# Pooled attention and a squared-relu feed-forward in one kernel: the squares of two short chunks move from VectorE to ScalarE, relu comes first in a step, the sums of w_in are spread over eight stages, and the attention of a chunk begins up to four steps sooner

## The chip, the cores and the metric

The kernel runs on one core of a Trainium2 chip. The metric is device time in microseconds (us). A core has five engines that run side by side, each working off its own queue in order: TensorE (PE in the profile, its weight loads PEld), VectorE (DVE), ScalarE (ACT), GpSimd (POOL) and SyncE (SP), which here issues every DMA. They wait for each other through semaphores. An instruction that waits holds up everything behind it in its own queue.

## The reference

```python
k_p = k.reshape(B, H, Sp, 8, D).mean(axis=3)          # B=8 batches, H=8 heads, S=576, D=64, Sp=72
v_p = v.reshape(B, H, Sp, 8, D).mean(axis=3)
scores = np.matmul(q, k_p.transpose(0, 1, 3, 2)) / np.sqrt(D)
attn = np.exp(scores - np.max(scores, axis=-1, keepdims=True))
attn = attn / (np.sum(attn, axis=-1, keepdims=True) + 1e-09)
x = np.matmul(attn, v_p).transpose(0, 2, 1, 3).reshape(B * S, H * D)   # 4608 tokens of 512
h = np.maximum(x @ w_in, 0.0)                                          # w_in 512 x 2048
out = h * h @ w_out                                                    # w_out 2048 x 512
```

## The kernel before

**Chunks and steps.** The 4608 tokens are worked off in ten chunks: 0 to 3 of 384 tokens (the short ones), 4 to 9 of 512. A chunk has 16 steps, one for each 128 columns of `w_in`; step s is step s % 16 of chunk s // 16. Every float32 product is made of three matmuls, with each operand split into a rounded high part and the rest (`gh` and `gl`, the two halves of `x`, `st`, `w_i`).

**A step of a short chunk.** `hidden(c, fc)` puts 12 matmuls into a PSUM bank `h` (two of these banks, shared with `pc` and `pd` below). `activate()` then takes relu and square of the bank into `r`: relu on ScalarE, the square on ScalarE in chunks 0 and 1 and on VectorE in 2 and 3. In the next step `split_hidden` makes `gh` (ScalarE) and `gl` (VectorE) from `r`, and three steps later (two in chunks 0 and 1) `project` multiplies them with `w_out` into the banks `o` (9 matmuls); the weights `ws` come back from DRAM for each step. In the code before, `activate()` is called last in a step, behind all of that step's attention work.

**Long chunks.** From chunk 4 on (`SC = 4`) the hidden layer is computed with a scheme of seven products instead of eight: two steps make one group of columns, with seven products of 6 matmuls (`pc`, `pd`, `pe`), whose operands are blocks of the chunk's `x` (`B11`, `T1` and so on, made by `difference` and `operands`) and sums of blocks of `w_in` (`S1` to `S4`, tile `w_s`). `build(g, stage)` makes these sums for four groups of columns out of `w_i` and scratch tiles `u`: `combine` adds on VectorE, `high` casts on ScalarE, `low` subtracts on VectorE. `first_half` (even steps) and `second_half` (odd steps) write the order of products out by hand. In `first_half` the bank `pc` of the first product is copied to `r1` by ScalarE, and the product with `S2` is then added into the same bank, so TensorE has to wait for that copy.

**Attention ahead of time.** The attention of chunk c runs in the steps of the chunks before it, in four pairs of heads. A pair is a list of stages: `turn_q` (VectorE), `split_q` (ScalarE casts, VectorE subtracts, tile `st`), `scores_0` and `scores_1` (TensorE, bank `sps`, one of two `a` banks; then a copy to `sc` on ScalarE and a maximum `mx` over partitions on GpSimd), `exponents` (VectorE subtracts the maximum, ScalarE takes exp, GpSimd sums: `tot`), `send_sums`, `reciprocals`, `send_reciprocals`, `fetch_reciprocals` (a round trip through DRAM: `rc`, `rr`, `rd`, `rb`), `weigh_values` (TensorE, bank `av`, then a copy to `xf` on ScalarE or to `x`) and `normalise`. Pooled keys make such a trip too (`kp`, `kd`, `kt`), and `turn_k` then turns and splits them (`kf`, `kh`, `kl`).

**What sets the order.** Tables of numbers: `FIRST_OF` and `STEADY` give the step, counted from the start of the chunk, from which each pair runs; `STAGES` and `STEADY_STAGES` give the offset of each stage; `KV_OF` and `KV_STEADY` the steps of keys and values; `BUILD` the first step of each `build`. Within a step the calls come in a fixed order: TensorE's work of the step, then the streams of `ws`, the evictions of the scores and values (`later`), the operands, the end of a pair of steps (`finish`), and all other stages in `others()`:

```python
        for f in later:
            f()
        if c < SC:
            urgent()
        if finish:
            finish()
        if c < SC or "t" not in (ORDER_A, ORDER_B)[fc % 2]:
            others()
```

Each engine's queue is then exactly this program order; only the buffers behind the names are given out by the framework.

Of the kernel before, what the change touches and what calls it, by code (L numbers as in the profile page):

```python
# [37 lines left out]
def pooled_attn_relu2_ffn(  # L38
# [24 lines left out]
    NPAIR = H // 2  # L63
# [13 lines left out]
    SC, MC = 4, 2  # L77
    LAG, FLAG, QL = 2, 3, 4
# [1 line left out]
    IDLE = (10, 3)  # L80
    STB, SCB, LD, XB, RB = 1, 3, 2, 7, 3
    ORDER_A, ORDER_B = "1ooo265uao", "7oo3uooa4"
    BUILD, RING = (36, 45, 64, 69), 2


    FIRST, EAGER, AHEAD = 4, 10, 4
    PRO, RATE, MARGIN = 5, 2, 1
# [2 lines left out]


    EARLY = (-16, -13, -10, -6)
    FIRST_OF = {2: (-18, -15, -11, -8), 3: (-20, -17, -13, -10)}
    STEADY = (-24, -20, -16, -12)
    STAGES = {c: (-1, 0, 1, 1, 3, 4, 5, 5, 5, 7) for c in (2, 3)}
    STEADY_STAGES = [(-2, -1, 1, 2, 3, 5, 6, 7, 8, *x) for x in ((11, 12), (8, 9), (7, 9), (7, 9))]
    NKT = H * SP_ // QT
    KV_OF = {3: ((-34, -33, -32, -31, -30, -29), -28, -27, -26, (-26, -25, -24, -23, -22, -21), -20, -19),
             4: ((-32, -31, -30, -29, -28, -27), -26, -26, -24, (-24, -23, -22, -21, -20, -19), -18, -17)}
    KV_STEADY = ((-31, -30, -30, -29, -29, -28), -28, -26, -24, (-24, -23, -22, -21, -20, -19), -18, -17)  # L100
    WC = 256

    const = ctx.enter_context(tc.tile_pool(name="const", bufs=1))
# [482 lines left out]
    def hidden(c, fc):  # L586
        hp = ps_h.tile([P, 512], F32, name=f"h_{c}_{fc}", tag="h")
        cb, o = fc * P // WC, fc * P % WC
        prods = []
        for cc in range(NCC):  # L590
            key, cols = ("i", cb, cc // 2 * 2), slice(cc % 2 * WC + o, cc % 2 * WC + o + P)
            if c == 0 and fc < SPLIT:
                prods += [(wf[key][:, cols], x0[cc // 2][:, cc % 2, :])]
            else:
                prods += [(wt[key][:, w, cols], xts[c][cc][:, x, :]) for w, x in ((0, 0), (0, 1), (1, 0))]
        for i, (w, x) in enumerate(prods):
            PE.matmul(hp[:, :SIZES[c]], lhsT=w, rhs=x, start=i == 0, stop=i == len(prods) - 1)

        def activate():
            if c == 0:  # L600
                r = sb.tile([P, SIZES[c]], F32, name=f"r_{c}_{fc}", tag="gh", bufs=LAG + 1)
            else:
                r = sb.tile([P, SIZES[c]], F32, name=f"r_{c}_{fc}", tag="r", bufs=RB)
            ACT.activation(r, hp[:, :SIZES[c]], AF.Relu)
            if c < 2:
                ACT.activation(r, r, AF.Square)
            else:
                DVE.tensor_tensor(r, r, r, op=ALU.mult)
            gts[c, fc] = r

        return activate
# [22 lines left out]
    def build(g, stage):  # L634
        a11, a12, a21, a22 = (wt["i", g + 4 * r, 2 * k] for r in range(2) for k in range(2))
        hi, lo = (lambda t: t[:, 0, :].bitcast(F32)), (lambda t: t[:, 1, :].bitcast(F32))

        def high(n, src):
            t = wt["s", n, g] = w_tile(F32R, f"w_s{n}_{g}")
            ACT.copy(t[:, 0, :], src)  # L640

        def low(n, src):
            t = wt["s", n, g]
            DVE.tensor_tensor(t[:, 1, :], src, hi(t), op=ALU.subtract)

        def combine(dst, first, second, add):
            DVE.tensor_tensor(dst, first, second, op=ALU.add if add else ALU.subtract)

        if stage == 0:
            us[g] = [half_tile("u", f"u{i}_{g}") for i in range(2)]  # L650
        u1, u2 = us[g]
        if stage == 0:
            combine(u1, hi(a21), lo(a21), True)
            combine(u2, hi(a22), lo(a22), True)
        elif stage == 1:
            combine(u2, u1, u2, True)
            high(1, u2)
        elif stage == 2:
            combine(u1, hi(a11), u1, False)
            combine(u1, u1, lo(a11), True)  # L660
            low(1, u2)
            high(3, u1)
        elif stage == 3:
            combine(u2, u2, hi(a11), False)
            combine(u2, u2, lo(a11), False)
            high(2, u2)
        elif stage == 4:
            low(3, u1)
            low(2, u2)
        elif stage == 5:  # L670
            combine(u2, hi(a12), u2, False)
            combine(u2, u2, lo(a12), True)
            high(4, u2)
        else:
            low(4, u2)
# [142 lines left out]
    def at(step, f, *a):  # L818
        work.setdefault(max(step, -PRO), []).append((f, a))
# [115 lines left out]
                at(k_turn, turn_k, b)  # L935
        at(v_fetch, fetch_rows, "v", b)

    ready = {0, 1}
    stages = (turn_q, split_q, scores_0, scores_1, exponents, send_sums, reciprocals, send_reciprocals, fetch_reciprocals, weigh_values, normalise)
    for c in range(1, NCH):  # L940
        first = EARLY if c == 1 else FIRST_OF.get(c, STEADY)
        offsets = [(0, 1, 2, 3, 5)] * NPAIR if c == 1 else [STAGES[c]] * NPAIR if c in STAGES else STEADY_STAGES
        names = (transpose_q, token_scores, token_normalise, token_turn, weigh_values) if c == 1 else stages
        for b, _, _ in segments(c):
            if b not in ready:
                ready.add(b)
                kv_steps(b, c)
        for p in range(NPAIR):
            s = c * NFC + first[p]
            if c > 1 or p:  # L950
                at(s - QL, load_q, c, p)
            for d, f in zip(offsets[p], names):
                at(s + d, f, c, p)

# [4 lines left out]
        if c >= MC:  # L959
            at(s - (4 if s < SC * NFC - 4 else RING), stream, c, f)  # L960
    for g, s in enumerate(BUILD):
        for stage in range(7):
            at(s + stage, build, g, stage)
    for c in range(SC, NCH):
        s = c * NFC
        for d, f, *names in ((-10, difference, "T1"), (-2, operands, "B11", "B21", "T1"), (-2, difference, "T2"),
                             (-2, operands, "T2"), (-1, difference, "T3"), (-1, operands, "T3"),
                             (-1, difference, "T4"), (-1, operands, "B22"), (0, operands, "T4")):
            at(s + d, f, c, *names)
# [3 lines left out]
    for s in range(-PRO, max(projects) + 1):  # L973
        todo = work.get(s, [])

        def on_array():
            return [f(*a) for f, a in sorted(((f, a) for f, a in todo if f in on_pe), key=lambda x: x[0] is weigh_values)]

        def urgent():
            for f, a in todo:  # L980
                if f in (operands, difference):
                    f(*a)

        def others():
            for f, a in todo:
                if f not in on_pe + last + (stream, operands, difference):
                    f(*a)

        groups = project(*projects[s]) if s in projects else iter(())
        activate = finish = None  # L990
        c, fc = steps[s] if 0 <= s < len(steps) else (0, 0)
        if c < SC:
            activate = hidden(c, fc) if 0 <= s < len(steps) else None
            later = on_array()
            for _ in groups:
                pass
            if 0 <= s - 1 < len(steps) and steps[s - 1][0] < SC:
                split_hidden(*steps[s - 1])
            if s == len(steps):
                high(NCH - 1, NQD - 1)  # L1000
                low(NCH - 1, NQD - 1)
                rest(NCH - 1, NQD - 1)
                low(NCH - 1, NFC - 1)
        else:
            qd = fc // 2
            pc, pq = (c, qd - 1) if qd else (c - 1, NQD - 1)
            before = (pc, pq) if pc >= SC else None
            if fc % 2:
                later, finish = second_half(c, qd, before, groups, on_array, urgent, others)
            else:  # L1010
                if pc < SC:
                    split_hidden(pc, NFC - 1)
                later = first_half(c, qd, before, groups, on_array, urgent, others)
        for f, a in todo:
            if f is stream:
                f(*a)
        for f in later:
            f()
        if c < SC:
# [5 lines that stand above are left out]
        keys = [a[0] for f, a in todo if f is to_float32]  # L1025
        if keys:
            to_float32(*keys)
        for f, a in todo:
            if f is split_weights:
                f(*a)  # L1030
        issue_loads()
        if activate:
            activate()
# [30 lines left out]
```

## Time and profile before

| | |
|---|---|
| median of three runs | 1056.6 us (1050.52 to 1059.32) |
| profiled execution: time, span | 1054.14 us, 1052.4 us |
| mean granted TensorE clock | 0.951 |
| TensorE busy | 942.4 us (90%) |
| VectorE busy | 689.2 us (65%) |
| ScalarE busy | 500.3 us (48%) |
| GpSimd busy | 345.0 us (33%) |

In the lines of the profile below, a group of instructions reads: engine, operation, tiles written <- tiles read, shapes, count, busy time and mean duration, then the idle time of the engine in front of them and what ended it ("<-ACT r" is an instruction of ScalarE on tile `r`). All lines of this kernel carry the number L34, that of a recording helper, so instructions are told apart by their tiles. Tile names lose their buffer numbers: `h`, `pc`, `pe`, `r`. PEclk is the share of its full clock that TensorE was granted. A busy TensorE also runs slower where that share is below 1.

### The profile page before, as it was taken

To read this page: it belongs to the slowest core of one execution; us is meant where nothing else is said; L and a number is where in the kernel's file an instruction comes from. 1 tells how busy PE (TensorE), PEld (TensorE's weight loads), DVE (VectorE), ACT (ScalarE), POOL (GpSimd) and SP (SyncE) were. 2 spreads that over 40 slices of the span, in tenths; PEclk is the share of its full clock that TensorE was granted. 3 is DMA by queue.
4 is the path that set the end of the run, shared out by engine and by line. 5 is a ranking of instruction groups with operands and counts; after the bars stand their busy time and mean duration, and the time that the engine had idled before them with its cause. 6 is when DMAs were issued, how large, how long until landed. Compare 5 with 4: busy or idle time off the path is not lost.

```text
span 1052.4 us, 14702 instructions
## 1 busy us (share of the span) xinstructions
PE 942.4 (90%) x5256; PEld 784.2 (75%) x5256; DVE 689.2 (65%) x1076; ACT 500.3 (48%) x1035; POOL 345.0 (33%) x183
## 2 busy tenths in 40 slices
PE   7899989988887887877779987999799979999998
PEld 6557667876766776766668876887688868888997
DVE  6989776666776577777767667777756565435332
ACT  2897755543343333434345445544554445435333
POOL 4800143443443444223334432443234434300000
PEclk9999999998988988888889999999999999999999
DMA  9953244576364545242435554555443434434701
GB/s 261 340 179 90 66 141 140 189 196 157 104 173 124 133 127 157 94 112 74 117 87 171 146 129 116 171 136 141 106 141 101 123 79 141 120 111 135 286 1 41
DMA packets 144753, 143.54 MB, mean 136 GB/s; under 512 B 98536, under 2 KB 103784, under 8 KB 144680
## 3 DMA queue, kind: packets, MB, share of 16 engines
q1 hardware_dynamic: 144680, 142.60, 46.8%
q8 instruction: 41, 0.67, 0.3%
q14 instruction: 32, 0.26, 0.1%
HBM read 122.72 MB, written 19.72 MB: 135 GB/s over the span
## 4 chain that ended last, share of the span: by engine, by line
PE 36%; DVE 8%; ACT 4%; DMA 3%; issue 1%; SPq 1%; DVEq 0%; ACTq 0%
PE o L34 17%; PE pc L34 9%; PE pe L34 5%; PE pd L34 2%; DVE gl L34 2%; DVE st L34 1%; DVE r L34 1%; PE av L34 1%; DMA vd<-vp 1%; PE sps L34 1%; ACT st L34 1%; DVE xf L34 1%; ACT sc L34 1%; ACT r L34 1%; DMA ws<-wd 1%
## 5 line engine op out<-in xcount | busy, mean ns | idle before, releaser
L34 PE MATMUL o<-ws,gh 128*128 128x512 f32 x960 | 310.4, 405 | 5.6 <-DMA ws<-wd 5.6
L34 POOL PARTITION_ALL_REDUCE tot<-sc x64 | 199.0, 3155 | 150.9 <-ACT sc L34 148.0
L34 POOL PARTITION_ALL_REDUCE mx<-sc x64 | 113.3, 1790 | 406.0 <-DMA rc<-tot 194.9
L34 PEld LDWEIGHTS o<-ws,gh 128*128 128x128 f32 x960 | 171.7, 195 | 36.4 <-issue 6.4
L34 PE MATMUL o<-ws,gl 128*128 128x512 f32 x480 | 191.6, 399 | 2.8 <-DVE gl L34 2.8
L34 PE MATMUL h<-x,w_i 128*128 128x384 f32 x696 | 143.9, 357 | 21.7 <-ACT r L34 21.7
L34 DVE TENSOR_TENSOR gl<-r,gh 128x512 fp32r<-128x512 f32 (+1 forms) x144 | 121.7, 845 | 56.6 <-ACT gh L34 55.0
L34 PEld LDWEIGHTS h<-x,w_i 128*128 128x128 f32 x696 | 129.1, 197 | 34.6 <-ACT r L34 25.4
L34 PE MATMUL pc<-T,w_s 128*128 128x256 f32 x576 | 92.5, 300 | 35.3 <-ACT r L34 35.1
L34 ACT CAST gh<-r 128x512 fp32r<-128x512 f32 (+1 forms) x144 | 84.2, 585 | 77.1 <-DVE r L34 67.5
L34 PEld LDWEIGHTS pc<-T,w_s 128*128 128x128 f32 x576 | 85.4, 206 | 42.4 <-ACT r L34 37.9
L34 PEld LDWEIGHTS o<-ws,gl 128*128 128x128 f32 x480 | 92.8, 193 | 26.6 <-DVE gl L34 5.5
L34 DVE TENSOR_TENSOR st<-qt,st 64x512 fp32r<-64x512 f32 (+1 forms) x64 | 70.0, 1094 | 47.7 <-ACT st L34 46.6
L34 DVE TENSOR_TENSOR r<-pd,r 128x256 f32<-128x256 f32 x48 | 20.3, 423 | 97.8 <-PE pd L34 96.1
L34 ACT COPY r<-pc 128x256 f32<-128x256 f32 x96 | 35.7, 372 | 86.6 <-PE pc L34 86.2
L34 ACT ACTIVATE r<-r 128x512 f32<-128x512 f32 (+2 forms) x128 | 67.3, 526 | 2.5
L34 ACT COPY sc<-sps 72x512 f32<-72x512 f32 (+1 forms) x64 | 34.6, 552 | 48.6 <-PE sps L34 48.5
L34 ACT ACTIVATE sc<-sc 72x512 f32<-72x512 f32 (+1 forms) x64 | 36.6, 601 | 33.1 <-DVE sc L34 33.1
L34 PE MATMUL pc<-T,w_i 128*128 128x256 f32 x288 | 44.8, 291 | 6.7 <-DVE r L34 6.6
L34 PEld LDWEIGHTS pc<-T,w_i 128*128 128x128 f32 x288 | 38.2, 189 | 15.6 <-DVE r L34 10.1
L34 PEld LDWEIGHTS pd<-B,w_i 128*128 128x128 f32 x288 | 41.0, 192 | 11.4 <-ACT r L34 8.1
L34 PE MATMUL pd<-B,w_i 128*128 128x256 f32 x288 | 43.0, 286 | 6.8 <-ACT r L34 6.8
(117 smaller groups left out, 1473.3 us busy)
## 6 DMA issues: line engine op xcount, KB each, us to landing
ws<-wd SPq DMA_DIRECT2D x128, 512.0 KB
k<-in_k_dram SPq DMA_DIRECT2D x48, 192.0 KB
out_dram<-ob SPq DMA_DIRECT2D x36, 256.0 KB
raw_i<-in_moe_w_in_dram SPq DMA_DIRECT2D x16, 512.0 KB
raw_o<-in_moe_w_out_dram SPq DMA_DIRECT2D x16, 512.0 KB
wd<-w_o SPq DMA_DIRECT2D x16, 512.0 KB
v<-in_v_dram SPq DMA_DIRECT2D x36, 192.0 KB
rb<-rd SPq DMA_DIRECT2D x48, 128.0 KB
```

What stands on the lines that cost most here:

```text
L34: return lambda *a, **k: self.tc.keep_in_program_order(f(*a, **k))
```

## The change

The squares of chunks 2 and 3 are taken by ScalarE's Square. In the short chunks except the first, `activate()` is called right behind the streams, ahead of `later` and `others()`. `build` has eight stages instead of seven: a cast of ScalarE now stands a stage, and so a step, behind the sum that it reads. `BUILD` starts two of the four builds one or two steps sooner. The tables of the attention start pairs up to four steps sooner (`FIRST_OF` gets an entry for chunk 4), turn and split the queries of chunks 2 and 3 one step sooner relative to the scores, and fetch and turn pooled keys up to two steps sooner. A load of queries is not put ahead of the step in which the tile before it is turned.

```diff
-    BUILD, RING = (36, 45, 64, 69), 2
+    BUILD, RING = (36, 45, 62, 68), 2
-    STEADY = (-24, -20, -16, -12)
+    STEADY = (-26, -22, -18, -14)
...
             ACT.activation(r, hp[:, :SIZES[c]], AF.Relu)
-            if c < 2:
+            if c < SC:
                 ACT.activation(r, r, AF.Square)
             else:
                 DVE.tensor_tensor(r, r, r, op=ALU.mult)
...
         elif stage == 1:
             combine(u2, u1, u2, True)
+            combine(u1, hi(a11), u1, False)
+        elif stage == 2:
             high(1, u2)
-        elif stage == 2:
-            combine(u1, hi(a11), u1, False)
             combine(u1, u1, lo(a11), True)
+        elif stage == 3:
+            high(3, u1)
             low(1, u2)
-            high(3, u1)
-        elif stage == 3:
             combine(u2, u2, hi(a11), False)
             combine(u2, u2, lo(a11), False)
+        elif stage == 4:
             high(2, u2)
-        elif stage == 4:
             low(3, u1)
+        elif stage == 5:
             low(2, u2)
-        elif stage == 5:
             combine(u2, hi(a12), u2, False)
             combine(u2, u2, lo(a12), True)
+        elif stage == 6:
             high(4, u2)
         else:
             low(4, u2)
...
-                at(s - QL, load_q, c, p)
+                at(max(s - QL, turned), load_q, c, p)
+                turned = s + offsets[p][0]
...
         for f, a in todo:
             if f is stream:
                 f(*a)
+        if activate and c:
+            activate()
+            activate = None
         for f in later:
             f()
```

The first place is ScalarE's queue in chunk 3, around the exponents of the last pair of chunk 4 (`sc_3`): steps 53 to 55. Before, with the relu of a step behind that step's exponents and query casts:

```order
L34 CAST gh_5_3335<-r_5_3305 128x384
L34 COPY sc_3_3297<-sps_3_1_3321 72x512
L34 ACTIVATE r_6_3360<-h_6_3308 128x384
L34 CAST gh_6_3391<-r_6_3360 128x384
L34 COPY xf_2_3376<-av_2_3377 128x512
L34 ACTIVATE sc_3_3297<-sc_3_3297 72x512 x2
L34 CAST st_0_3408<-qt_0_3357 64x512 x2
L34 ACTIVATE r_7_3413<-h_7_3363 128x384
```

The same exponents in ScalarE's queue after the change:

```order
L34 CAST gh_4_3310<-r_4_3268 128x384
L34 ACTIVATE r_5_3316<-h_5_3283 128x384
L34 ACTIVATE r_5_3316<-r_5_3316 128x384
L34 COPY xf_0_3126<-av_1_3296 128x512
L34 ACTIVATE sc_3_3218<-sc_3_3218 72x512 x2
L34 CAST st_0_3338<-qt_0_3280 64x512 x2
L34 CAST gh_5_3371<-r_5_3316 128x384
L34 ACTIVATE r_6_3377<-h_6_3343 128x384
L34 ACTIVATE r_6_3377<-r_6_3377 128x384
```

The relu of a step now stands ahead of the exponents and casts of that step, the square (`r<-r`) stands behind it on ScalarE, and the exponents of this pair come two steps sooner.

The second place is ScalarE's queue where chunk 5 begins (step 79 into step 80). Before, with the exponents of a pair of chunk 6 (`sc_1`) and the casts of the next pair (`st_2`) in the last step of chunk 4:

```order
L34 CAST T_5_4880<-xf_0_4054 128x512
L34 CAST B_5_4884<-xf_2_4342 128x512
L34 ACTIVATE r_15_4819<-pc_7_4775 128x256
L34 ACTIVATE sc_1_4763<-sc_1_4763 72x512 x2
L34 CAST st_2_4915<-qt_2_4857 64x512 x2
L34 COPY r_0_4929<-pc_0_4922 128x256
```

The same place after the change:

```order
L34 CAST T_5_4907<-xf_0_4025 128x512
L34 CAST B_5_4911<-xf_2_4316 128x512
L34 COPY sc_2_4933<-sps_2_0_4920 72x512
L34 ACTIVATE r_15_4847<-pc_7_4803 128x256
L34 COPY r_0_4953<-pc_0_4946 128x256
```

Between the relu of the old chunk's last group and the copy `r<-pc` of the new chunk's first, the exponents and the casts are gone (they now stand in steps 77 and 81); a copy of scores has come ahead of the relu.

The third place is ScalarE's queue in chunk 4, around the sums for the third group of columns (`w_s_2` is the cast `high`). Before, steps 67 into 68:

```order
L34 ACTIVATE r_9_3988<-pc_1_3939 128x256
L34 ACTIVATE sc_2_3922<-sc_2_3922 72x512 x2
L34 CAST st_3_4082<-qt_3_4008 64x512 x2
L34 CAST w_s_2_4092<-u_2_3875 128x512
L34 COPY r_2_4102<-pc_2_4095 128x256
```

After the change, the same exponents, steps 65 into 66:

```order
L34 ACTIVATE r_8_3892<-pc_0_3852 128x256
L34 ACTIVATE sc_2_3828<-sc_2_3828 72x512 x2
L34 CAST st_3_3960<-qt_3_3910 64x512 x2
L34 CAST w_s_2_3968<-u_2_3781 128x512
L34 COPY r_1_3981<-pc_1_3974 128x256
```

The queue reads alike, but the sum `u` that the cast reads was made in the same step before and is made in the step ahead of it now.

More of the change, by code (lines that the diff above doesn't have):

```diff
@@ L92, in pooled_attn_relu2_ffn @@
     EARLY = (-16, -13, -10, -6)
-    FIRST_OF = {2: (-18, -15, -11, -8), 3: (-20, -17, -13, -10)}
-    STEADY = (-24, -20, -16, -12)
-    STAGES = {c: (-1, 0, 1, 1, 3, 4, 5, 5, 5, 7) for c in (2, 3)}
-    STEADY_STAGES = [(-2, -1, 1, 2, 3, 5, 6, 7, 8, *x) for x in ((11, 12), (8, 9), (7, 9), (7, 9))]
+    FIRST_OF = {2: (-18, -15, -11, -8), 3: (-21, -17, -14, -11), 4: (-24, -21, -18, -14)}
+    STEADY = (-26, -22, -18, -14)
+    STAGES = {2: [(-2, -1, 1, 1, 3, 4, 5, 5, *x) for x in ((6, 7), (6, 7), (6, 8), (6, 7))],
+              3: [(-2, -1, 1, 1, 3, 4, *x) for x in ((5, 6, 6, 9), (5, 6, 6, 8), (6, 6, 7, 9), (6, 6, 7, 9))]}
+    STAGES[4] = [(-2, -1, 1, 2, 3, 5, 6, 7, *x) for x in ((8, 10, 11), (8, 10, 11), (8, 8, 9), (8, 9, 10))]
+    STEADY_STAGES = [(-2, -1, 1, 2, 3, 5, 6, 7, *x) for x in ((8, 12, 13), (9, 11, 12), (8, 8, 9), (8, 9, 10))]
     NKT = H * SP_ // QT
-    KV_OF = {3: ((-34, -33, -32, -31, -30, -29), -28, -27, -26, (-26, -25, -24, -23, -22, -21), -20, -19),
-             4: ((-32, -31, -30, -29, -28, -27), -26, -26, -24, (-24, -23, -22, -21, -20, -19), -18, -17)}
-    KV_STEADY = ((-31, -30, -30, -29, -29, -28), -28, -26, -24, (-24, -23, -22, -21, -20, -19), -18, -17)
+    KV_OF = {3: ((-34, -33, -32, -31, -30, -29), -28, -27, -25, (-26, -25, -24, -23, -22, -21), -20, -19),
+             4: ((-32, -31, -31, -30, -30, -29), -29, -28, -26, (-24, -23, -22, -21, -20, -19), -18, -17)}
+    KV_STEADY = ((-31, -30, -30, -29, -29, -28), -28, -27, -26, (-24, -23, -22, -21, -20, -19), -18, -17)
     WC = 256
@@ L936, in kv_steps @@
         at(v_fetch, fetch_rows, "v", b)
-    ready = {0, 1}
+    ready, turned = {0, 1}, -PRO
     stages = (turn_q, split_q, scores_0, scores_1, exponents, send_sums, reciprocals, send_reciprocals, fetch_reciprocals, weigh_values, normalise)
@@ L941, in pooled_attn_relu2_ffn @@
         first = EARLY if c == 1 else FIRST_OF.get(c, STEADY)
-        offsets = [(0, 1, 2, 3, 5)] * NPAIR if c == 1 else [STAGES[c]] * NPAIR if c in STAGES else STEADY_STAGES
+        offsets = [(0, 1, 2, 3, 5)] * NPAIR if c == 1 else STAGES.get(c, STEADY_STAGES)
         names = (transpose_q, token_scores, token_normalise, token_turn, weigh_values) if c == 1 else stages
@@ L961, in pooled_attn_relu2_ffn @@
     for g, s in enumerate(BUILD):
-        for stage in range(7):
+        for stage in range(8):
             at(s + stage, build, g, stage)
@@ L965, in pooled_attn_relu2_ffn @@
         s = c * NFC
-        for d, f, *names in ((-10, difference, "T1"), (-2, operands, "B11", "B21", "T1"), (-2, difference, "T2"),
+        for d, f, *names in ((-9, difference, "T1"), (-2, operands, "B11", "B21", "T1"), (-2, difference, "T2"),
                              (-2, operands, "T2"), (-1, difference, "T3"), (-1, operands, "T3"),
```

## The prediction

> **What bounds the kernel now.** I read the stretches first, one for each chunk that the change touches, and beside them stretches of the same chunks in which TensorE never stops.
>
> ```profile
> span 1052.4 us, 14702 instructions
> core 0: us, PE busy (x) PEld busy (x) DVE busy (x) ACT busy (x) POOL busy (x), PEclk, DMA share, GB/s
> 129.17:211.51 82.34, 77.41 (x365) 63.47 (x364) 56.97 (x87) 46.62 (x95) 32.58 (x17) 0.98 0.50 160
> 148.60:176.41 27.81, 27.81 (x139) 23.68 (x138) 19.84 (x30) 14.11 (x29) 11.23 (x6) 1.00 0.58 178
> 211.51:311.09 99.58, 82.33 (x373) 68.46 (x372) 71.05 (x103) 36.70 (x75) 42.88 (x20) 0.90 0.58 154
> 311.09:409.30 98.21, 82.01 (x401) 69.92 (x399) 67.16 (x91) 36.54 (x71) 41.43 (x16) 0.93 0.48 134
> 381.15:409.30 28.15, 27.86 (x147) 24.32 (x145) 20.71 (x28) 11.29 (x22) 14.07 (x6) 1.00 0.60 169
> 409.30:542.06 132.76, 104.34 (x583) 89.71 (x584) 93.65 (x136) 53.82 (x109) 40.61 (x16) 0.86 0.38 105
> 498.06:510.29 12.23, 12.23 (x80) 10.41 (x79) 10.81 (x17) 5.38 (x12) 3.88 (x2) 1.00 0.49 131
> 542.06:560.02 17.96, 13.35 (x73) 11.78 (x72) 14.07 (x18) 8.10 (x16) 7.98 (x3) 0.81 0.36 99
> 665.99:678.32 12.33, 12.33 (x80) 10.41 (x79) 8.05 (x12) 6.50 (x15) 3.56 (x2) 1.00 0.66 201
> 856.98:874.47 17.49, 12.87 (x71) 11.23 (x70) 13.08 (x17) 8.09 (x16) 7.97 (x3) 0.90 0.33 82
> ```
>
> The rows at 129.17, 211.51, 311.09 and 409.30 are chunks 1, 2, 3 and 4 whole. The row at 148.60 is six consecutive steps of chunk 1 and that at 381.15 the last six of chunk 3 (six times 21 matmuls of the hidden layer are 126; the rest of the 139 and 147 is attention): 27.81 / 6 = 4.64 us and 28.15 / 6 = 4.69 us a step with TensorE full at full clock, attention included. The row at 498.06 is such a pair of steps of chunk 4, that at 665.99 one of chunk 6. The rows at 542.06 and 856.98 are the first pair of chunks 5 and 8, the first and the last of four alike (chunks 5 to 8).
>
> So where TensorE isn't stopped it is the bound, and the cost of a chunk is its clean steps plus stops. At clean steps chunk 1 would be 16 x 4.64 = 74.2 us, chunks 2 and 3 16 x 4.69 = 75.1 each, chunk 4 8 x 12.23 = 97.8, a first pair 12.3. Each loss has two parts. Chunk 2 is 24.5 us over: TensorE stands idle for 99.58 - 82.33 = 17.3, and its busy time is 82.33 instead of 75.1, which goes with the granted clock of 0.90 there. Chunk 3 is 23.1 over (16.2 idle, 6.9 slower busy time), chunk 4 34.9 (28.4 and 6.5), chunk 1 8.2 (4.9 and 3.2). So a stop costs about 1.4 times its length.
>
> Second, the waits, with sum, count and longest, to see what the stops are.
>
> ```profile
> PE pc L34 <- ACT r L34: 35.4, 11, 6.3
> PE h L34 <- ACT r L34: 21.7, 8, 6.2
> PE sps L34 <- DVE st L34: 12.6, 5, 4.2
> PE o L34 <- DMA ws<-wd: 5.6, 2, 4.7
> ACT gh L34 <- DVE r L34: 67.5, 26, 7.4
> DVE gl L34 <- ACT gh L34: 55.0, 60, 5.3
> ACT w_s L34 <- DVE u L34: 41.4, 12, 5.3
> POOL mx L34 <- DMA rc<-tot: 194.9, 25, 14.4
> ```
>
> TensorE waits mostly for ScalarE's `r`, though ScalarE is busy only 48%: `r` is not slow, it stands behind instructions that themselves wait for VectorE.
>
> **The change part by part.** *Relu first.* The window at the start of chunk 4 shows the stop at its longest; the last two rows, some steps earlier, are a sum of GpSimd with a square inside it:
>
> ```profile
> 418.59 0.49 ACT L34 ACTIVATE r<-h 128x384 f32<-128x384 f32 x1
> 419.14 1.65 PE L34 MATMUL pd<-B,w_i 128*128 128x256 f32 x6 [6.81 <-ACT r L34]
> 367.76 6.60 POOL L34 PARTITION_ALL_REDUCE tot<-sc  x2 [2.31 <-ACT sc L34]
> 371.30 2.48 DVE L34 TENSOR_TENSOR r<-r 128x384 f32<-128x384 f32 x1
> ```
>
> The relu at 418.59 empties the bank of chunk 3's last step and is 0.49 us long; `pd` takes that bank and has stood for 6.81 us. Once the relu leads its step, the bank is free about 0.5 us behind its last matmul, and the exponents behind it delay no bank. This answers the 21.7 us of `h` and the 6.81.
>
> *Squares.* What goes from VectorE and comes to ScalarE:
>
> ```profile
> L34 DVE TENSOR_TENSOR r<-r 128x384 f32<-128x384 f32 x32 | 25.6, 799 | 7.6 <-ACT r L34 7.4
> L34 ACT ACTIVATE r<-r 128x384 f32<-128x384 f32 x32 | 16.8, 525 | 1.0
> ```
>
> Sixteen squares a chunk leave VectorE: 16 x 0.80 = 12.8 us, so chunk 2 has 58.3 us of it left in 75.1 and chunk 3 54.4. ScalarE takes 16 x 0.525 = 8.4 more: 45.1 in chunk 2, 60% of 75.1. Chunk 1 already runs so, with ScalarE 14.11 busy in its clean 27.81. I cost the squares at nothing: `gh` is needed two to three steps after the bank is read, so the 0.525 lies beside TensorE; without that cover it would be 32 x 0.525 = 16.8. What it saves is the round trip ScalarE, VectorE, ScalarE, the 67.5 us that `gh` waits for `r`, part of which becomes the stops on `h`.
>
> The square at 371.30 took 2.48 us, inside the GpSimd sum from 367.76 to 374.36, against a mean of 0.80. The Trainium skill, "SBUF — State Buffer", section "Who interferes with whom", says that a VectorE instruction with two SBUF inputs contends with a GpSimd instruction that reads SBUF, and that the other one blocks. The overlap here agrees. By this rule the blocking isn't removed with the square but falls on the next two-input instruction (`gl`, `st`, `kl`); the ScalarE time of 0.525 as the unblocked size leaves 32 x (0.80 - 0.525) = 8.8 us, and the forecast would be that much higher if all of it stood in front of TensorE.
>
> *Sums of `w_in` in eight stages.*
>
> ```profile
> 452.98 0.62 ACT L34 CAST w_s<-u 128x512 fp32r<-128x512 f32 x1 [5.26 <-DVE u L34]
> 453.51 0.36 ACT L34 COPY r<-pc 128x256 f32<-128x256 f32 x1
> 453.93 1.65 PE L34 MATMUL pc<-T,w_s 128*128 128x256 f32 x6 [6.34 <-ACT r L34]
> 516.32 2.62 DVE L34 TENSOR_TENSOR w_s<-u,w_s 128x512 fp32r<-128x512 f32 x1
> 519.00 0.34 SPq L34 DMA_DIRECT2D ws<-wd  x1
> 522.73 1.22 PE L34 MATMUL o<-ws,gh 128*128 128x512 f32 x2 [4.75 <-DMA ws<-wd]
> 524.03 4.04 SPq L34 DMA_DIRECT2D q<-in_q_dram  x8
> ```
>
> ScalarE reached the cast and stood 5.26 us for a sum of the same step; the 0.36 us copy of `pc` behind it kept TensorE 6.34 us. A like stop falls at 482. With the sum a step ahead, the cast finds it done. What could be late next is the sum's own start: two builds start one or two steps sooner and one stage longer, on a VectorE that works 10.81 of 12.23 us in the clean pair. Of a stage, as many sums, casts and differences are issued as before. The stop at 518 is a stream of `ws` issued at 519.00, behind the difference that ended at 518.94: that difference stood behind exponents and queries in step 75, which now stand in 73 and 77. All three stops go in my sum.
>
> *Attention sooner.* Pairs shift so that exponents and query splits fall on steps 1, 5, 9, 13 of a chunk instead of 3, 7, 11, 15.
>
> ```profile
> 547.56 1.23 ACT L34 ACTIVATE sc<-sc 72x512 f32<-72x512 f32 x2 [2.82 <-DVE sc L34]
> 548.70 1.24 ACT L34 CAST st<-qt 64x512 fp32r<-64x512 f32 x2
> 549.97 0.37 ACT L34 COPY r<-pc 128x256 f32<-128x256 f32 x1
> 550.39 1.65 PE L34 MATMUL pc<-T,w_s 128*128 128x256 f32 x6 [4.62 <-ACT r L34]
> ```
>
> Here a chunk's first copy of `pc` stands behind exponents, which wait for VectorE, and casts of the step before it; four chunks pay for it with about 17.7 - 12.3 = 5.4 us each, 21.6 in all. Exponents of step 77 are done a pair before that copy. Of a later pair the same work then stands in step 1 (odd), where no copy of `pc` is waited for by the first product; I cost it at nothing, as in the middle of the chunk, where the clean pair at 665.99 runs.
>
> Moved along are the DMAs. SP issues a load of queries in 4.04 us (eight DMAs), and streams of `ws` queue behind it. Streams come first in a step, and the load stays two steps ahead of its use. Between nothing and the 4.75 us of the row at 522.73 for each load, I take nothing, since a single such stop exists now. GpSimd's maxima and sums come with the pairs; their number stays. The copy of `av` into `xf` falls into the step of the output stores:
>
> ```profile
> 678.23 0.59 ACT L34 COPY xf<-av 128x512 f32<-128x512 f32 x1 [3.17 <-DMA out_dram<-ob]
> 377.21 0.36 PE L34 MATMUL sps<-st,kl 128*72 128x256 f32 x1 [3.06 <-DVE kl L34]
> ```
>
> It already waits 3.17 us for a store, on a ScalarE with idle time; one step earlier it waits longer, and may then hold the relu or copy of the next step. Between nothing and the 3.17 us again in front of TensorE, once a chunk, I take nothing, as the row at 678.23 lies in a stretch that TensorE runs through. Pooled keys are turned two steps sooner and their scores too, so the trip through DRAM gets no longer lead: the 3.06 us of `kl` stays or doubles.
>
> *Sum.* Chunk 1 -8.2, chunk 2 -24.5, chunk 3 -23.1, chunk 4 -34.9, four first pairs -21.6: together -112.3. The profiled execution took 1054.1 us (1.7 over its span), so 941.8 if no stop were left in these places. The four rows of TensorE's waits hold 26 waits; 112.3 / 26 = 4.3 us for each, clock included. I leave six: the pooled keys of chunk 4, the head of chunk 4 (two schemes meet there), and four, one in each of chunks 1 to 4, where VectorE's blocked instruction meets a new neighbour. 941.8 + 6 x 4.3 = **968 us**. The six are a choice, between none (942) and half of the 26 (998). The profiled execution lies 0.2% under the median of 1056.6 and within the runs, so I don't shift the sum.
>
> **The rivals.** *VectorE becomes the bound.* For it: chunk 4 has 93.65 us of VectorE's time and a clean length of 97.8, 96%, and instructions that GpSimd blocks. Against it: the clean pairs ran with 10.81 of 12.23 beside full TensorE, and chunk 2 would be at 78%. If half of the loss in chunks 2 to 4 stays: 41.3 back on 941.8, 983; with two of the six other waits 992.
>
> *ScalarE's longer queue is what TensorE waits for.* The square now stands ahead of score copies and `gh`; if that costs chunks 2 and 3 what they gain, 941.8 + 47.6 = 989. Against it stands chunk 1, clean with the square on ScalarE. The Trainium skill, "ScalarE: Activation LUTs", section "Rules for kernel authors", tells one to take relu and multiplications on VectorE rather than ScalarE. The rows here have 525 ns on ScalarE and 799 on VectorE in this form, so the trace doesn't bear it out.
>
> *Attention does not start sooner.* GpSimd's maxima wait 194.9 us in 25 waits for an earlier pair's sums on their way through DRAM. If that trip, not the tables, sets the pace, exponents stay where they are beside the first pairs, and half of chunk 4's loss with them: 941.8 + 21.6 + 17.5 = 981.
>
> *Slower.* The loads of queries come, in chunks 0 to 4, to stand in front of the stream that TensorE needs next. From the point where a stream's lead falls under the load's 4.04 us, each of 20 loads costs the 4.75 us of the row at 522.73 times 1.4, 6.6: 968 + 132 = 1100. Against it: one such stop now among 40 loads.
>
> **How the numbers follow.** The forecast 0.62, VectorE 0.18, ScalarE 0.10, attention 0.06, slower 0.04. The range from 940 (no stop left) to 1005 (half of the stops left, 998, and a late store or two) holds the first four but for tails. A measurement of this kernel cannot tell less than about 1% from no change; within it I put 0.02, slower 0.04, faster 0.94.
>
> **What would show it.** Chunks 2 and 3 within 76 to 84 us each, at a clock above 0.95; chunk 4 at 98 to 107; first pairs of chunks 5 to 8 at 12.3. In the waits, `h` for `r`, `gh` for VectorE's `r` and `w_s` for `u` should be nearly gone; VectorE about 25 us less busy, ScalarE 17 more. Wrong if TensorE's waits for `st`, `kl` or `gl` grow to tens of us (VectorE), if `h` or `sps` waits for ScalarE's `r` or `sc` (its queue), if first pairs keep 17.7 (attention), or if `o` waits for `ws` in many steps (loads).

## The result and the profile after

The changed kernel takes **982.6 us** (median of three, 979.77 to 984.56) against 1056.6 before: ratio 0.9307, 95% interval 0.9233 to 0.938. The forecast was 968, the range 940 to 1005. In the profiled executions TensorE stands idle for 978.1 - 920.7 = 57.4 us instead of 110.0, and its 5256 matmuls take 920.7 us instead of 942.4, at a mean granted clock of 0.984 instead of 0.951. So 52.6 us less of stops came with a span shorter by 74.3, 1.4 times as much, the factor that the prediction had taken.

The same views of the changed kernel: first the page's head, then the stretches of chunks 1, 2, 3, 4 and 5 (the columns are those of the table in the prediction), the first pairs of steps of chunks 5 and 8, and TensorE's waits with VectorE's and ScalarE's beside them.

```profile
span 978.1 us, 14676 instructions
PE 920.7 (94%) x5256; PEld 766.4 (78%) x5256; DVE 674.8 (69%) x1044; ACT 510.5 (52%) x1067; POOL 345.2 (35%) x183
129.90:205.31 75.41, 75.25 (x365) 62.53 (x363) 60.34 (x89) 47.85 (x101) 37.67 (x18) 1.00 0.57 177
205.31:282.91 77.60, 75.19 (x376) 64.53 (x375) 58.09 (x87) 40.84 (x86) 38.12 (x18) 0.98 0.70 185
282.91:371.46 88.55, 79.18 (x402) 67.59 (x400) 65.73 (x76) 45.48 (x89) 47.76 (x19) 0.96 0.54 155
371.46:486.73 115.27, 99.67 (x585) 84.84 (x584) 93.87 (x135) 54.48 (x111) 42.97 (x17) 0.94 0.46 127
486.73:589.14 102.41, 96.02 (x595) 81.77 (x594) 75.86 (x106) 50.78 (x104) 40.99 (x16) 1.00 0.51 144
486.73:498.16 11.43, 11.31 (x73) 9.87 (x72) 8.81 (x15) 6.00 (x13) 3.17 (x2) 1.00 0.42 138
788.50:799.98 11.48, 11.35 (x70) 9.62 (x69) 9.28 (x17) 6.00 (x13) 3.10 (x2) 1.00 0.14 51
...
ACT gh L34 <- DVE r L34: 10.7, 5, 2.4
PE o L34 <- DVE gl L34: 9.9, 11, 2.9
PE pc L34 <- ACT r L34: 9.1, 12, 3.9
PE pc L34 <- DVE r L34: 7.3, 6, 1.6
PE o L34 <- DMA ws<-wd: 4.4, 3, 1.9
PE sps L34 <- ACT xf L34: 4.1, 1, 4.1
PE sps L34 <- DVE st L34: 2.9, 2, 2.0
PE sps L34 <- DVE kl L34: 2.9, 2, 2.5
ACT w_s L34 <- DVE u L34: 2.3, 2, 1.7
```

Chunks 1 and 2 are now at the pace of their clean steps: TensorE is idle for 0.2 and 2.4 us. The waits of `pc` for ScalarE's `r` fell from 35.4 to 9.1 us, that of `h` for `r` (21.7) is gone from the list, that of ScalarE's cast `w_s` for `u` fell from 41.4 to 2.3 and that of `gh` for VectorE's `r` from 67.5 to 10.7. But chunk 3 still has 88.55 - 79.18 = 9.4 us of idle TensorE and chunk 4 15.6, and two waits of TensorE are new or larger: `o` for `gl` (2.8 us before) and `sps` for the copy into `xf` (none before). These are the places, from the timeline (start, duration, engine, instruction, idle time before it):

```profile
303.60 1.38 SPq L34 DMA_DIRECT2D out_dram<-ob  x3
308.58 0.58 ACT L34 COPY xf<-av 128x512 f32<-128x512 f32 x1 [6.03 <-DMA out_dram<-ob]
309.22 0.44 PE L34 MATMUL sps<-st,kl 128*72 128x192 f32 x1 [4.05 <-ACT xf L34]
...
380.47 0.36 ACT L34 COPY r<-pc 128x256 f32<-128x256 f32 x1
380.88 1.65 PE L34 MATMUL pc<-T,w_s 128*128 128x256 f32 x6 [3.93 <-ACT r L34]
...
447.09 2.43 DVE L34 TENSOR_TENSOR st<-qt,st 64x512 fp32r<-64x512 f32 x2 [1.21 <-ACT st L34]
449.54 2.64 DVE L34 TENSOR_TENSOR w_s<-u,w_s 128x512 fp32r<-128x512 f32 x1
452.21 0.69 DVE L34 TENSOR_TENSOR u<-w_i,u 128x512 f32<-128x512 f32 x1
452.94 0.69 DVE L34 TENSOR_TENSOR u<-u,w_i 128x512 f32<-128x512 f32 x1
453.55 0.41 DVE L34 TENSOR_TENSOR r<-pd,r 128x256 f32<-128x256 f32 x1
453.88 0.68 DVE L34 TENSOR_TENSOR gl<-r,gh 128x512 fp32r<-128x512 f32 x1
454.62 0.80 PE L34 MATMUL o<-ws,gl 128*128 128x512 f32 x1 [2.90 <-DVE gl L34]
...
485.91 0.98 PE L34 MATMUL pc<-T,w_i 128*128 128x256 f32 x6 [1.58 <-DVE r L34]
```

At 308.58 ScalarE's copy into `xf` stood 6.03 us for the output stores: in the kernel `ob`, which they read, and `xf` take turns in the same two buffers. The scores, which need the bank that this copy empties, stood 4.05. At 453.88 `gl` stands in VectorE's queue behind the query split and three operations of a stage of the `w_in` sums. The last row is a short stop in the last step of chunk 4, which comes back at the end of chunks 5 to 7; before, the same stops were 0.93 to 1.31 us long. The row at 380.88 is the head of chunk 4, one of the six stops that the forecast left.

### The profile page after: what moved, and what is told of

Its sections match the earlier page's. It is cut to its first block, busy times and chain, and to the rows that moved or that the text cites. A ratio compares the mean times of both kernels' runs of the same rounds, so it can differ in the third digit from the quotient of the medians.

```text
span 978.1 us, 14676 instructions
## 1 busy us (share of the span) xinstructions
PE 920.7 (94%) x5256; PEld 766.4 (78%) x5256; DVE 674.8 (69%) x1044; ACT 510.5 (52%) x1067; POOL 345.2 (35%) x183
## 4 chain that ended last, share of the span: by engine, by line
PE 55%; DVE 20%; ACT 8%; DMA 7%; issue 5%; SPq 3%; POOL 1%; DVEq 0%; ACTq 0%
PE o L34 26%; PE pc L34 9%; PE h L34 8%; DVE gl L34 5%; PE pe L34 4%; SPq L34 3%; DVE st L34 3%; PE av L34 3%; DVE r L34 2%; PE sps L34 2%; DMA k<-in_k_dram 2%; PE pd L34 2%; ACT r L34 2%; ACT sc L34 2%; ACT st L34 2%
## 5 line engine op out<-in xcount | busy, mean ns | idle before, releaser
L34 POOL PARTITION_ALL_REDUCE mx<-sc x64 | 113.8, 1799 | 366.7 <-DMA rc<-tot 193.3
L34 DVE TENSOR_TENSOR gl<-r,gh 128x512 fp32r<-128x512 f32 (+1 forms) x144 | 130.5, 906 | 28.3 <-ACT gh L34 26.9
L34 PE MATMUL h<-x,w_i 128*128 128x384 f32 x696 | 136.6, 345 | 0.0
L34 PEld LDWEIGHTS h<-x,w_i 128*128 128x128 f32 x696 | 123.9, 188 | 9.9 <-issue 4.8
L34 PE MATMUL pc<-T,w_s 128*128 128x256 f32 x576 | 87.4, 288 | 9.2 <-ACT r L34 9.1
L34 ACT CAST gh<-r 128x512 fp32r<-128x512 f32 (+1 forms) x144 | 84.2, 585 | 18.1 <-DVE r L34 10.7
L34 PEld LDWEIGHTS pc<-T,w_s 128*128 128x128 f32 x576 | 79.3, 193 | 17.2 <-ACT r L34 13.4
L34 DVE TENSOR_TENSOR st<-qt,st 64x512 fp32r<-64x512 f32 (+1 forms) x64 | 66.0, 1031 | 38.7 <-ACT st L34 37.5
L34 ACT ACTIVATE r<-r 128x384 f32<-128x384 f32 (+2 forms) x160 | 84.1, 526 | 3.5
L34 DVE TENSOR_TENSOR r<-pd,r 128x256 f32<-128x256 f32 x48 | 20.2, 421 | 83.8 <-PE pd L34 83.4
L34 ACT ACTIVATE r<-pc 128x256 f32<-128x256 f32 x48 | 18.4, 383 | 81.9 <-PE pc L34 81.7
L34 PE MATMUL pc<-T,w_i 128*128 128x256 f32 x288 | 44.1, 289 | 7.3 <-DVE r L34 7.3
L34 ACT COPY r<-pe 128x256 f32<-128x256 f32 x48 | 17.9, 373 | 62.5 <-DVE gl L34 53.5
L34 DVE TENSOR_REDUCE kp<-k 96x64 f32<-96x512 f32 x42 | 43.5, 1054 | 7.6 <-DMA k<-in_k_dram 7.4
```

What stands on the lines that cost most here:

```text
L34: return lambda *a, **k: self.tc.keep_in_program_order(f(*a, **k))
```

## The experiments

Twelve kernels, each timed in four runs, with its own runs of the kernel before on the same chip. Totals are compared through those. Lengths of chunks come from one profiled execution each, from the first product of a chunk to the first of the next; they leave out the time ahead of chunk 0's first product, which wandered between 41.1 and 44.1 us (50.9 in the last kernel) whatever was changed. The length of a chunk wanders too: chunk 2 has the same instructions in the same order in the changed kernel and in the three kernels "sums a step later", "values a step later" and "both later", and took 77.6, 80.1, 79.2 and 78.2 us. So a difference of 2 to 3 us in one chunk means nothing, and one of about 4 is weak evidence.

| kernel | ratio to before (95%) | chunk 1 | 2 | 3 | 4 | 5 to 8 |
|---|---|---|---|---|---|---|
| before | | 82.3 | 99.6 | 98.2 | 132.8 | 413.1 |
| the change | 0.931 (0.923 to 0.938) | 75.4 | 77.6 | 88.5 | 115.3 | 394.3 |
| relu first alone | 0.983 (0.977 to 0.988) | 85.8 | 92.5 | 90.5 | 126.8 | 412.7 |
| squares alone | 0.985 (0.981 to 0.990) | 81.9 | 95.3 | 91.7 | 126.3 | 412.9 |
| eight stages alone | 0.980 (0.975 to 0.984) | 83.5 | 93.6 | 93.0 | 121.3 | 415.1 |
| attention tables alone | 0.964 (0.960 to 0.968) | 75.4 | 98.1 | 103.0 | 119.4 | 393.5 |
| all but relu first | 0.932 (0.929 to 0.936) | 75.4 | 82.6 | 91.1 | 110.8 | 396.2 |
| all but the squares | 0.943 (0.940 to 0.947) | 75.4 | 83.6 | 95.6 | 116.2 | 395.6 |
| all but eight stages | 0.942 (0.937 to 0.946) | 75.4 | 82.0 | 92.0 | 122.9 | 396.2 |
| all but the tables | 0.964 (0.961 to 0.967) | 86.6 | 87.4 | 83.7 | 116.2 | 415.7 |
| sums a step later | 0.931 (0.928 to 0.934) | 75.4 | 80.1 | 90.1 | 115.0 | 394.1 |
| values a step later | 0.931 (0.929 to 0.934) | 75.4 | 79.2 | 92.5 | 114.4 | 393.8 |
| both later | 0.928 (0.925 to 0.932) | 75.4 | 78.2 | 92.6 | 111.1 | 393.3 |
| both, relu last | 0.931 (0.926 to 0.935) | 75.4 | 82.4 | 92.3 | 107.5 | 394.7 |

**One part alone.** Each of these four kernels takes one piece of the diff over into the kernel before; the lines below are the first of the pieces. Theory: every part removes its own stops. Rival: the parts work only together.

```diff
+        if activate and c:            # relu first alone
+            activate()
+            activate = None
         for f in later:
```

> The kernel before with one part of the change: relu first in the step of chunks 1 to 3 (the squares of chunks 2 and 3 stay on VectorE, right behind the relu). Theory (each part takes away its own stops): the 21.7 us of h waiting for r and the 6.81 us at 412 go, times 1.4, so about 40 us, 1016. Rival (the parts work only together: with the square still in VectorE's queue and exponents late, the stops move to gl and st): under 12 us, above 1044.

1037.4 us against 1057.6: 20 us, between theory and rival. TensorE's waits in this kernel:

```profile
PE pc L34 <- ACT r L34: 37.5, 10, 6.4
PE sps L34 <- DVE st L34: 23.4, 8, 4.7
PE sps L34 <- DVE kl L34: 7.3, 2, 5.1
```

The 21.7 us of `h` for `r` are gone from the head of the list, as the theory has it; but the scores' wait for `st` grew from 12.6 to 23.4: half of what was gained is waited for one engine further on.

> The kernel before with the squares of chunks 2 and 3 on ScalarE alone, relu and square still last in a step. Theory: the relu stays behind exponents and query casts, so the stops of h stay; only the round trip over VectorE is shorter: 10 us or less, about 1047. Rival (the round trip itself was the cause): the 67.5 us that gh waits for r shrink and the stops of h with them, 25 us or more, under 1032.

1041.4: 16 us, again between. It brought more than the theory said, in chunks 2 to 4 (17 us of the profiled execution), with the relu still behind the exponents.

> The kernel before with the sums of w_in in eight stages (and the start of two builds at steps 62 and 68) alone. Theory: the stops at 447 and 482 go (6.34 + 5.37, times 1.4 = 16 us), the one at 518 as well if the difference no longer meets the queries: 16 to 23 us, 1034 to 1040. Rival (VectorE is behind in chunk 4 anyway): the copies go ahead but gl comes late, under 6 us.

1033.8: 24 us, the theory's upper end; chunk 4 gives 11.5, and chunks 2 and 3, in which the first two builds run, 11.2 more, of which the theory had said nothing.

> The kernel before with the tables of the attention alone (pairs up to four steps sooner, query splits of chunks 2 and 3 a step sooner, pooled keys sooner, difference T1 a step later). Theory: the first pairs of chunks 5 to 8 lose 21.6 us and the waits of scores for st 12.6 x 1.4 = 18, relu still stands behind exponents: 35 to 40 us, about 1019. Rival (the trip of the sums through DRAM sets the pace): no change of the first pairs, under 12 us.

1017.7: 40 us, the theory's upper end. Chunk 1 (-6.9) and chunks 5 to 8 (-19.6) have their whole gain from the tables. Yet chunk 3 became 4.8 us *longer*. Attention work of chunk 4 comes into it while the relu still stands behind it, and in this kernel `h` waits 24.1 us for ScalarE's `r` (21.7 before); that this alone makes up the 4.8 is not shown.

The four gains add up to 100 us; together they gave 74.

**All but one part.** Four kernels take one piece back out of the changed one.

> The changed kernel with relu and square put last in a step again. Theory (each part its own stops): loses what the part alone gains on the kernel before, some 30 to 40 us, so about 1015. Rival (with the exponents moved and the squares off VectorE, the order within a step matters little): under 10 us, below 993.

The ratio is that of the whole change (0.932 and 0.931): relu first brings nothing any more once the other three are there. The rival holds. Chunks 2 and 3 lose 7.6 us and chunk 4 wins 4.5. Part of this only crosses the border between two chunks: TensorE's stop at the head of chunk 4 (2.53 us at 377.17) now lies ahead of that chunk's first product, and so is counted in chunk 3. The place at 305 shows how one cause takes another victim:

```profile
309.83 0.59 ACT L34 COPY xf<-av 128x512 f32<-128x512 f32 x1 [7.02 <-DMA out_dram<-ob]
310.32 0.50 ACT L34 ACTIVATE r<-h 128x384 f32<-128x384 f32 x1
310.87 2.61 PE L34 MATMUL h<-x,w_i 128*128 128x384 f32 x7 [5.51 <-ACT r L34]
```

The copy waits for the stores as in the changed kernel; with the relu behind it, it is the hidden layer that stands, not the scores.

> The changed kernel with the squares of chunks 2 and 3 on VectorE again, relu still first. Theory: TensorE's bank is free with the relu, so at most 10 us are lost, about 990. Rival (VectorE is what chunks 2 and 3 wait for after the change): gl and st come later, 20 us or more, above 1002.

Worse by 0.943 - 0.931 = 1.2% of 1053, 13 us: between the two, in chunks 2 and 3 (6.0 and 7.0 us longer).

> The changed kernel with the sums of w_in in seven stages from steps 64 and 69 again. Theory: two or three stops of 5 to 6 us come back in chunk 4, times 1.4: 15 to 23 us, about 1000. Rival (the tight place of chunk 4 is VectorE's queue, and the later builds relieve it at steps 65, 69 and 73): under 5 us, or a gain.

Also 12 us worse. Chunk 4 is 7.6 longer, not the theory's 15 to 23: of TensorE's waits, `pc` for ScalarE's `r` rises from 9.1 to 15.3 and `o` for `gl` falls from 9.9 to 6.3.

```profile
PE pc L34 <- ACT r L34: 15.3, 11, 5.4
PE o L34 <- DVE gl L34: 6.3, 10, 2.0
```

So part of the rival is true: the eight stages, with two builds started at steps 62 and 68, buy the removed stops with new ones on VectorE, 3.6 us of them. This profiled execution is the slowest of its four (997.4 us, median 992.3), so the 7.6 may be too long by some us.

> The changed kernel with the tables of the attention of before. Theory: first pairs of chunks 5 to 8 return to 17.7 us (21.6 us), the waits for st come back (18 us), while the 4.05 us stop of scores behind the copy into xf at 305 goes (about 6): 30 to 35 us, about 1015. Rival (trip of the sums sets the pace): under 12 us.

35 us worse, as the theory says (chunks 1 and 5 to 8: 32.6 of it), and chunk 3 is 4.8 *better* than with the tables.

**The stops that are left.** Two edits to the changed kernel, and both together:

```diff
-            at(s + stage, build, g, stage)
+            at(s + stage + (s + stage in (65, 69, 73)), build, g, stage)
```
```diff
-    STAGES[4] = [... for x in ((8, 10, 11), (8, 10, 11), ...
+    STAGES[4] = [... for x in ((8, 11, 12), (8, 10, 11), ...
```

> The changed kernel with three stages of the sums of w_in, which fell into steps 65, 69 and 73 beside exponents and query splits, put one step later (into 66, 70, 74). Theory (in chunk 4 VectorE's queue is late by the three operations of such a stage, and gl behind them): the three stops of o for gl (1.88, 1.46, 2.90 us) go, times 1.4: 8.7 us, about 974. Rival (the split of queries that GpSimd blocks makes gl late, not the sums; or the sums then delay the next step's copy): under 3 us.

No gain: 0.931. The stops of `o` for `gl` at their old places are gone, and others stand elsewhere. The longest of them behind chunk 4's head is this one:

```profile
432.27 0.68 DVE L34 TENSOR_TENSOR w_s<-u,w_s 128x512 fp32r<-128x512 f32 x1
432.87 0.68 DVE L34 TENSOR_TENSOR u<-u 128x512 f32<-128x512 f32 x1
433.59 0.69 DVE L34 TENSOR_TENSOR u<-w_i,u 128x512 f32<-128x512 f32 x1
434.31 0.69 DVE L34 TENSOR_TENSOR u<-u,w_i 128x512 f32<-128x512 f32 x1
434.92 0.42 DVE L34 TENSOR_TENSOR r<-pc,r 128x256 f32<-128x256 f32 x1
435.39 1.65 PE L34 MATMUL pc<-T,w_i 128*128 128x256 f32 x6 [2.59 <-DVE r L34]
```

The four sum operations of step 70 now stand ahead of the addition `r<-pc,r`, which the next product into that bank waits for. So the sums do make VectorE late, but a step later they are as much in the way.

> The changed kernel with the values of the first pair of chunk 4 weighed and normalised one step later (step 51 instead of 50, out of the step of the output stores). Theory: the stop of 4.05 us of the scores in chunk 3, behind the copy into xf that waits for the stores, goes: 5.7 us, about 977. Rival (the next thing late takes its place, the pooled keys at 327 or the first products of chunk 4): under 2 us.

No gain: 0.931. The stop at 305 is gone, and the scores' stop for the pooled keys, 2.54 us in the changed kernel, is 5.50 here, as the rival has it. (In the kernel with the sums a step later, which has no edit in chunk 3, that stop was 4.36 us, so a part of the growth may be chance.) The kernel with both edits shows the place in full:

> Both: sums of steps 65, 69 and 73 a step later, and the first pair's values of chunk 4 a step later. If they add, 14 us: about 968; if one wait takes the other's place, 975 or more.

```profile
324.88 6.60 POOL L34 PARTITION_ALL_REDUCE tot<-sc  x2 [2.09 <-ACT sc L34]
325.93 2.45 DVE L34 TENSOR_TENSOR st<-qt,st 64x512 fp32r<-64x512 f32 x2 [1.21 <-ACT st L34]
328.41 2.49 DVE L34 TENSOR_TENSOR gl<-r,gh 128x384 fp32r<-128x384 f32 x1
330.82 0.68 DVE L34 TENSOR_TENSOR xf<-xf,rb 128x512 f32<-128x512 f32 x1
331.43 0.77 DVE L34 STREAM_TRANSPOSE kf<-kt 128x576 f32<-128x576 f32 x1
332.93 0.76 DVE L34 TENSOR_TENSOR kl<-kf,kh 128x576 fp32r<-128x576 f32 x1 [0.74 <-ACT kh L34]
333.74 0.49 PE L34 MATMUL sps<-st,kl 128*72 128x256 f32 x1 [5.51 <-DVE kl L34]
```

The DMAs that fetch the keys were issued from 323.99 to 326.20, and `kf` began at 331.43, as soon as VectorE had worked off the query split, a `gl` of 2.49 us inside GpSimd's sum, and `xf`. Chunk 4 is about 4 us shorter than in the changed kernel, chunk 3 about 4 longer. 978.7 us in the median; its interval overlaps that of the change, so it is not shown to be faster.

> As the kernel with both moves, and relu and square of the short chunks put last in a step again. Theory now (once squares are on ScalarE and exponents sooner, the order in the step decides only which of two waits stands in front of TensorE): within 5 us of the kernel with both moves. Rival (relu first was hidden only by the stop at the copy into xf): 6 us or more slower.

0.931 against 0.928, intervals overlapping, as the theory has it. TensorE stops elsewhere (`h` waits 12.9 us for ScalarE's `r`, against 0.4 in the kernel with both edits), and a difference in all is not shown.

## Why the prediction was right, and where its sum was off

**The bound and its stops: right.** Where nothing stops TensorE a chunk takes its clean steps: chunk 1 75.4 us against the 74.2 worked out, chunk 2 77.6 against 75.1, within the 76 to 84 that the prediction named as its sign. Chunk 3 (88.5) lies above the 84, and chunk 4 (115.3) above the 107 named for it. The first pairs, at 11.4 to 11.6, even lie below the 12.3 that was worked out for them.

**The sum, term by term.** The forecast is 968 against 978.1 + 1.7 = 979.8 for the profiled execution, 12 us too low. With the six stops of 4.3 us put where the text puts them, the terms were: chunk 1 -3.9, chunk 2 -20.2, chunk 3 (one stop and the pooled keys) -14.5, chunk 4 (one stop and its head) -26.3, first pairs -21.6. Measured: -6.9, -22.0, -9.7, -17.5, -18.9 (chunks 5 to 8 whole). Chunks 1 and 2 came out 5 us better, chunk 3 5 us and chunk 4 9 us worse, chunks 5 to 8 3 us worse. The six stops were a choice, as the prediction says, and misses of both signs met in the sum: 37 us of the 112.3 stayed where 26 had been left. That the total came within 1.5% is in part luck.

**The mis-sized terms.** First, the copy into `xf` one step earlier, behind the output stores, was costed at nothing because TensorE ran through such a wait in the kernel before; it stood 6.03 us and cost TensorE 4.05. Second, chunk 4: beside its head three stops are `gl` behind the split and the sums (1.88, 1.46 and 2.90 us), where one stop had been left. The condition was named (VectorE 96% of the clean length), then set aside for clean pairs, the one in chunk 4 with 10.81 of 12.23 us; that pair held neither exponents with a blocked split nor a stage of three operations at once. So the rival "VectorE becomes the bound" holds in chunk 4, in part: 17.5 of its 34.9 us of loss stayed, half, as that rival priced it, though the sign that was named for it did not show (the waits for `st`, `kl` and `gl` are 15.7 us together, 18.9 before). Third, in chunks 5 to 8 the first pairs gained more than was forecast, 6.3 us each instead of 5.4: the 12.3 was taken from clean pairs of 80 matmuls, and the rows of the first pairs count only 70 to 73. But behind the first pairs the four chunks became 6.5 us longer, 4.6 of it idle TensorE. There the wait of `pc` for ScalarE's copy rose from 1.1 to 4.0 us and that of `o` for `ws` from 0.9 to 2.6. One of these stops, in the second and third step of chunk 5:

```profile
502.45 0.37 ACT L34 COPY r<-pc 128x256 f32<-128x256 f32 x1
502.88 0.97 PE L34 MATMUL pc<-T,w_s 128*128 128x256 f32 x6 [1.07 <-ACT r L34]
```

This copy stood behind exponents and query casts that ScalarE ran from 500.04 on: the work that was moved into step 1 of a chunk, and costed at nothing there, is waited for too.

**Each part its own stops: only half right.** The prediction gave each part the waits it names. The runs show that relu first gives 20 us alone and nothing on top of the rest, and that a stop removed at one place is often replaced by one at the next thing VectorE owes. The four parts gain 20, 16, 24 and 40 us alone; taken out of the whole they cost 0, 13, 12 and 35. So much of what one part removes another removes too, or a new stop takes back; no run follows the missing 26 us stop by stop.

**Squares.** They were costed at nothing on ScalarE, and 25 us less of VectorE was foretold; the whole changed kernel has 689.2 - 674.8 = 14.4 less. (ScalarE is busy 10.2 us more, where 17 were foretold; with the squares alone it was 18.1.) The kernel with the squares alone, 668.9 us of VectorE, shows where a part of the rest went. Groups by form, `gl` of the short chunks in the kernel before and in that one (count, busy time, mean ns, idle before):

```profile
L34 DVE TENSOR_TENSOR gl<-r,gh 128x384 fp32r<-128x384 f32 x48 | 32.6, 679 | 37.5 <-ACT gh L34 37.4
L34 DVE TENSOR_TENSOR gl<-r,gh 128x384 fp32r<-128x384 f32 x48 | 39.4, 820 | 39.1 <-ACT gh L34 38.9
```

The squares are away and `gl`, whose number and form are unchanged, takes 6.8 us more. In the kernel before, five of the 32 squares took over 0.8 us (four of them 2.49), and five of these 48 `gl`; with the squares away ten `gl` do, four of them 2.49 to 2.50. Every one of these overlaps a GpSimd sum or maximum over partitions. The Trainium skill ("SBUF — State Buffer", "Who interferes with whom") says that a VectorE instruction with two SBUF inputs contends with a GpSimd one that reads SBUF. The prediction concluded that without the square the next such instruction would be blocked instead, and had 8.8 us as the price. This run bears the conclusion out, with 6.8. (In the whole changed kernel two more such instructions are longer than before: `w_s<-u,w_s` by 4.1 us and `xf<-xf,rb` by 3.7.)

**The other rivals.** ScalarE's longer queue is out: with the squares back on VectorE chunks 2 and 3 are 13 us longer. The trip of the sums is out: GpSimd's maxima wait for it as before (193.3 us), and the first pairs are clean. The loads of queries are out: `o` waits for `ws` 4.4 us in all, 5.6 before.

## What to carry to other kernels

Work out the clean length of each stage first: it tells how much there is to win, and was right within 4% in the two chunks without other waits. Then give the waits behind one queue a common account: an in-order engine near its stage's length (here VectorE in chunk 4, 94 of 115 us) can hand a removed stop to the next instruction that depends on it, and the single gains of the four edits here did not add. Before costing a moved copy at nothing, see whether its buffer is still held by a transfer, and who needs the bank it frees.

## What the runs showed of the hardware

What a VectorE instruction with two SBUF inputs pays beside a GpSimd sum over partitions goes with the place and not with the instruction: `gl` of 128x384 takes 0.55 us, and 2.49 inside the sum at 324.88; `w_s` takes 0.68, and 2.64 at 449.54, inside a sum that ran from 446.04 to 452.62. With the squares alone moved away, most of what they had paid moved to `gl`. An addition with one input in a PSUM bank paid nothing: of the 48 `r<-pd,r` in the kernel before, 16 ran wholly inside such a sum, and none took over 0.43 us.
